# Grouped-query attention over a key-value cache: 512-column scores, block transposes on VectorE, a row maximum, and wo rows loaded apart

## The chip, the cores and the metric

The kernel runs on one core of one Trainium2 chip. The core has a matrix engine (TensorE, PE in the profile, whose weight loads are shown apart as PEld), a vector engine (VectorE, DVE), a scalar engine (ScalarE, ACT), GpSimd (POOL) and SyncE (SP), which here only issues DMA transfers. Sixteen DMA engines move data between the chip's main memory and the on-chip memory SBUF; the matrix engine writes to the accumulator memory PSUM. The metric is the device time of one execution in microseconds (us); smaller is better.

## The reference

```
B, Sq, D = 8, 4, 512;  Hq, Hkv, Sk, Dh = 32, 8, 2048, 128      # all bf16
q = (x @ wq) as [B, Hq, Sq, Dh]
scores = einsum("bhqd,bhkd->bhqk", q, k repeated 4 times) * Dh ** -0.5
p = softmax(scores, axis=-1)
o = einsum("bhqk,bhkd->bhqd", p, v repeated 4 times)
return o as [B, Sq, Hq * Dh] @ wo
```

Each of the 8 key-value heads serves 4 query heads, so a pair (batch, key-value head) has 16 query rows against 2048 keys. The inputs are 33.6 MB of keys, as much of values, 4.2 MB of wq and 4.2 MB of wo; x and the output are 32 KB each.

## The kernel before

The work is cut into 16 units (`units`, L81): unit u is one batch and one group of G = 4 key-value heads. A unit's keys are one transfer of 2 MB (`load_k`, L85), its values another (`load_v`, L93). SBUF partition g * 32 + s holds 64 consecutive keys of head g, 16 KB in all, so each transfer writes 128 partitions with one 16 KB run each.

For the scores the keys must stand with the 128 head dimensions on the partitions. `transpose_part` (L143) does a quarter of a unit (t = 0 to 3): it views two bf16 values as one 4-byte word, transposes 128x128 blocks on TensorE against a 4-byte identity (L151) into a PSUM buffer of the pool `psum_k` (3 buffers), and VectorE copies each half quarter, 1024 bf16 per partition, to the tile `kt` (L152). The two dimensions of a word stay side by side, so q is prepared once as a block form `q_bd` with e = 0 and 1 for the two halves of a word.

`scores` (L212) multiplies, for each head g, each e and each quarter t, a 32-column weight by 256 columns of `kt` (L221, 32 matmuls per unit). Four quarters go to four groups of 32 output partitions. ScalarE takes the exponential of each head's scores and gives the row sums (L229). No maximum is subtracted. `probs_to_keys` (L236) transposes the result on TensorE (L239, 8 per unit) and ScalarE copies four 32-partition pieces into `probs` (L245), which is zero where a key's head is not the query's head. `norms` (L252) sums the row sums over the partitions by a matmul with ones (L261) and takes the reciprocal (L269). `values` (L273) accumulates 64 matmuls with value blocks as weights (L278), and `finish` (L286) scales the result into `oT`.

At the end `to_tokens` (L295) and `to_wo_rows` (L303) bring a half of the heads into the row order in which wo was loaded, and `project` (L312) multiplies by wo. wo has four parts p of 1024 rows; partition q of a part holds 8 consecutive rows of it, r = 0 to 7.

The order of instructions on each engine is the order in the code (`manual_schedule`, L64). The loop at L323 runs stages n = 1 to 17. Stage n transposes unit n's keys, does the scores and probabilities of unit n - 1 and the norms and values of unit n - 2 (w). On TensorE stage n is: quarter 0, scores(n - 1), quarter 1, the norms matmul, quarter 2, values first half, quarter 3, the probability transposes, values second half.

All loads go through SyncE's queue. Keys and values have three buffers each, so a load of unit u is issued when unit u - 3 has been read (the last key transposes, or the last value matmul): `load_ready` at L351 stands at the end of each stage. wo uses the place in SBUF that wq had. Part 0 of wo is loaded as one transfer ahead of the values of unit 14 (L112), and parts 1, 2 and 3 follow the values of unit 15, part 3 in four pieces of 256 KB (L354). The last matmuls wait for the last piece; then ScalarE copies the sum out (L364) and two transfers store it.

## Time and profile before

| what | value |
|---|---|
| median of 3 runs | 190.44 us (190.15 to 190.62) |
| profiled execution: span | 188.4 us; its own time is not listed apart from its span |
| moved by DMA | 75.89 MB, 403 GB/s over the span |
| PE, DVE, ACT busy | 140.1, 103.5, 94.4 us |
| load of keys, of values: issue to landing (median) | 21.8 us, 25.3 us |

The span runs from the program's first instruction to its last; it is 2.0 us under the median of the runs. Busy time of an engine is an average over the whole span, so it does not tell which engine a stage waits for. "Issue to landing" includes the time that a transfer stands behind earlier ones in the queue. Besides the data queue the profile lists queues of kind "instruction": through these the engines get their own programs from main memory, on the same 16 DMA engines.

### The profile page before, as it was taken

How to read it: one execution, taken by the hardware profiler on the slowest of the kernel's cores; microseconds unless marked ns; L12 is line 12 of the kernel's file. 1: busy time of each engine (PE TensorE's matmuls, PEld its weight loads, DVE VectorE, ACT ScalarE, POOL GpSimd, SP SyncE). 2: the span in 40 equal slices, each digit the busy share in tenths (PEclk: the TensorE clock that was granted, in tenths of full speed). 3: DMA queues.
4: the chain of work that ended last, by engine and by line, in shares of the span. 5: the costliest groups of instructions: out<-in, count | busy, mean ns of one | idle time of the engine just before them, and what ended most of it. 6: DMA issues, size and time to landing. Idle time of an engine off the chain costs nothing.

```text
span 188.4 us, 5301 instructions
## 1 busy us (share of the span) xinstructions
PE 140.1 (74%) x2356; PEld 121.5 (65%) x2356; DVE 103.5 (55%) x189; ACT 94.4 (50%) x200; POOL 8.2 (4%) x11
## 2 busy tenths in 40 slices
PE   0290869797979777777777888879777777776681
PEld 0290357696968766767675878777767677665560
DVE  4082286777776656574747457575747565740120
ACT  2000243958476573646556093919292837468500
POOL 8800000000000000000000000000000000000000
PEclk9999678999999999999999699999999999999997
DMA  6998999999999999999999999999999999999940
GB/s 202 466 445 383 428 421 431 428 411 435 431 402 438 426 431 411 431 435 414 421 438 421 431 418 435 418 424 435 421 418 438 419 428 412 414 445 414 399 184 12
DMA packets 5926, 75.89 MB, mean 403 GB/s; under 512 B 688, under 2 KB 784, under 8 KB 1296
## 3 DMA queue, kind: packets, MB, share of 16 engines
q1 hardware_dynamic: 5856, 75.55, 95.2%
q8 instruction: 18, 0.29, 0.6%
q14 instruction: 4, 0.03, 0.0%
q10 hardware_dynamic: 48, 0.02, 0.0%
HBM read 75.53 MB, written 0.03 MB: 401 GB/s over the span
## 4 chain that ended last, share of the span: by engine, by line
DMA 69%; PE 23%; DVE 4%; ACT 1%; issue 1%; SPq 1%
DMA wo_sb<-in_wo_dram 25%; DMA k_sb<-in_k_cache_dram 21%; DMA v_sb<-in_v_cache_dram 14%; PE kp L151 11%; DMA x_sb<-in_x_dram 9%; PE o_ps L278 4%; PE s_ps L221 3%; DVE kt L152 3%; PE psq L176 2%; PE pt L239 1%; PE l_ps L261 1%; ACT q_bd L201 1%; DVE q_bd L201 0%; ACT q_nat L185 0%; DVE by_gq L254 0%
## 5 line engine op out<-in xcount | busy, mean ns | idle before, releaser
L152 DVE COPY kt<-kp 128x1024 bf16<-128x1024 bf16 x128 | 82.0, 682 | 42.7 <-PE kp L151 42.6
L245 ACT COPY probs<-pt 32x1024 bf16<-32x1024 bf16 x64 | 64.2, 1002 | 58.4 <-PE pt L239 57.2
L151 PE MATMUL kp<-ident,k_sb 128*128 128x128 f32 x512 | 71.5, 286 | 16.9 <-DMA k_sb<-in_k_cache_dram 16.6
L151 PEld LDWEIGHTS kp<-ident,k_sb 128*128 128x128 f32 x512 | 59.0, 148 | 22.3 <-issue 13.2
L278 PE MATMUL o_ps<-probs,v_sb 128*128 128x64 bf16 x1024 | 35.7, 195 | 4.4 <-DMA v_sb<-in_v_cache_dram 4.4
L278 PEld LDWEIGHTS <-v_sb 128*128 128x128 bf16 x1024 | 34.0, 99 | 5.2 <-DMA v_sb<-in_v_cache_dram 5.1
L229 ACT ACTIVATE s_sb<-s_ps 128x256 bf16<-128x256 f32 x64 | 23.6, 383 | 2.2 <-PE s_ps L221 1.9
L221 PE MATMUL s_ps<-kt,q_bd 128*32 128x256 bf16 x512 | 18.6, 286 | 0.0
L261 PE MATMUL l_ps<-by_gq,ones 128*128 128x64 f32 x32 | 6.9, 298 | 15.6 <-DVE by_gq L254 15.6
L261 PEld LDWEIGHTS l_ps<-by_gq,ones 128*128 128x128 f32 x32 | 4.8, 188 | 19.3 <-DVE by_gq L254 17.6
L221 PEld LDWEIGHTS <-q_bd 128*32 128x32 bf16 x512 | 12.7, 97 | 3.7 <-issue 2.6
L269 DVE RECIPROCAL r_sb<-l_ps 128x64 f32<-128x64 f32 x16 | 8.9, 557 | 9.0 <-PE l_ps L261 9.0
L229 ACT ACTIVATION_READ_ACCUMULATOR s_sb<-s_ps 128x1 f32 x64 | 13.2, 206 | 0.0
L288 DVE TENSOR_TENSOR oT<-o_ps,r_sb 128x64 bf16<-128x64 f32 x16 | 3.6, 224 | 16.1 <-PE o_ps L278 16.1
L185 ACT ACTIVATE q_nat<-psq 128x512 bf16<-128x512 f32 x2 | 1.2, 597 | 20.0 <-PE psq L176 20.0
L239 PE MATMUL pt<-ident,s_sb 128*128 128x128 bf16 x128 | 9.8, 219 | 0.3 <-ACT s_sb L229 0.3
L239 PEld LDWEIGHTS <-s_sb 128*128 128x128 bf16 x128 | 8.4, 98 | 0.6 <-ACT s_sb L229 0.5
L315 PE MATMUL out_ps<-wo_sb,oP 128*32 128x256 bf16 x64 | 4.5, 274 | 1.0 <-DMA wo_sb<-in_wo_dram 0.5
L364 ACT CAST out_sb<-out_ps 64x256 bf16<-64x256 f32 x1 | 0.4, 365 | 8.2 <-PE out_ps L315 8.2
L315 PEld LDWEIGHTS <-oP 128*32 128x32 bf16 x64 | 3.0, 96 | 2.0 <-issue 0.9
L176 PE MATMUL psq<-wq_sb,xT_sb 128*32 128x512 bf16 x32 | 3.5, 623 | 0.3 <-DVE xT_sb L169 0.3
L134 POOL MEMSET probs<- 128x4096 bf16 x1 | 3.5, 3511 | 0.0
(27 smaller groups left out, 29.1 us busy)
## 6 DMA issues: line engine op xcount, KB each, us to landing
k_sb<-in_k_cache_dram SPq DMA_DIRECT2D x16, 2048.0 KB, 21.8
v_sb<-in_v_cache_dram SPq DMA_DIRECT2D x16, 2048.0 KB, 25.3
wq_sb<-in_wq_dram SPq DMA_DIRECT2D x1, 4096.0 KB, 17.0
wo_sb<-in_wo_dram SPq DMA_DIRECT2D x3, 1024.0 KB, 23.7
wo_sb<-in_wo_dram SPq DMA_DIRECT2D x4, 256.0 KB, 22.3
x_sb<-in_x_dram SPq DMA_DIRECT2D x1, 32.0 KB, 16.7
out_dram<-out_sb SPq DMA_DIRECT2D x1, 16.0 KB, 1.4
out_dram<-out_sb ACTq DMA_DIRECT2D x1, 16.0 KB, 1.6
```

Source lines behind the costliest of these rows:

```text
L151: nc.tensor.transpose(kp[:, j, :], k4[:, w : w + 128], ident4[:, :])
L152: nc.vector.tensor_copy(out=kt[(u, t)][:, half * J // 2 : (half + 1) * J // 2, :, :].rearrange("k j s e -> k (j s e)"), in_=kp[:, :, :].re ...
L176: nc.tensor.matmul(psq[g * T : (g + 1) * T, :], lhsT=xT_sb[:, r, :], rhs=wq_sb[:, r, c0 : c0 + rep * Dh], start=(r == 0), stop=(r == R - 1),)
L221: nc.tensor.matmul(s_ps[t * 32 : (t + 1) * 32, g % 2, :, :], lhsT=q_bd[:, hq, e, g, b, :, :], rhs=kt[(u, t)][:, :, g * S : (g + 1) * S, e] ...
L229: nc.scalar.activation(out=s_sbs[u][:, :, g, :], in_=s_ps[:, g % 2, :, :], func=EXP, accum_out=l_sbs[u][:, g : g + 1],)
L239: nc.tensor.transpose(pt[:, j, :], s_sbs[u][:, j, :, :].rearrange("q g s -> q (g s)"), ident[:, :])
L245: nc.scalar.copy(out=pr[rows, :, g, :], in_=pt[rows, :, :].rearrange("s j (c q) -> s (j c) q", q=HQ),)
L261: nc.tensor.matmul(l_ps[:, :], lhsT=ones[:, :], rhs=by_gq[:, :, :].rearrange("k g q -> k (g q)"), start=True, stop=True,)
L269: nc.vector.reciprocal(r_sbs[u][:, :], l_ps[:, :])
L278: nc.tensor.matmul(o_pss[u][:, :], lhsT=vs[u][:, 2 * (t * J + j) + c, :], rhs=probs[u % 2][:, i, :, :].rearrange("s g q -> s (g q)"), star ...
L288: nc.vector.tensor_tensor(out=oT[hq][:, :, :, b, :].rearrange("d h p s -> d p h s"), in0=o_pss[u][:, :].rearrange("d (p h s) -> d p h s", ...
L315: nc.tensor.matmul(out_ps[half * T : (half + 1) * T, :], lhsT=oP[p // 2][:, r, p % 2, :], rhs=wo_sb[:, p, r, half * DH : (half + 1) * DH], ...
```

## The change

- SBUF is laid out anew: a pad of 384 bytes and the large buffers come first, the small tiles behind. In before the wq/wo, key and value buffers begin 192 bytes past a multiple of 512, in the changed kernel on a multiple of 512.
- The transposed keys are kept as two halves of a unit, 3 buffers of 8 KB in the place of 6 of 4 KB. Of each quarter's two copies VectorE does the first and ScalarE the second. `psum_k` has 4 buffers, the scores' pool one of two banks, and the pool of the probability transposes is gone.
- Scores: 16 matmuls of 512 columns in the place of 32 of 256, with the four heads on the four groups of output partitions. VectorE takes the row maximum over all 1024 scores of a partition, swaps it with the partition that holds the other half of the same row (stream_shuffle), and forms the negated maximum of both. One exponential per unit on ScalarE uses it as bias (new function `exponentials`).
- Probabilities: VectorE transposes 32x32 blocks of 4-byte words and copies four 32-partition pieces; TensorE and ScalarE do nothing there.
- Norms: the same, with one multiplication by a per-partition scalar.
- wo, part 0: the first 640 of its 1024 rows are loaded in two transfers (256 and 384 KB) whose outer dimension in main memory is 8, after the values of units 4 and 10; the other 384 rows keep the old place. `to_tokens` and `to_wo_rows` follow this order of rows for n = 0. The result of `to_wo_rows` is 4-byte in PSUM.
- In a stage the second half of the order is: quarter 1, exponentials, norms, values first half, quarter 2, probs_to_keys, quarter 3, values second half.

```diff
+    align = ctx.enter_context(tc.tile_pool(name="align", bufs=1))
+    align.tile([128, 192], BF16, name="pad")
...
     def load_wo(p, r0, n):
+        rows = wo[p * HP * 128 : (p + 1) * HP * 128, :]
+        if p == 0 and r0 < XR:
+            rows = rows[: 128 * XR, :].rearrange("(b a r) j -> a b r j", a=8, r=XR)
+            nc.sync.dma_start(wo_sb[:, p, r0 : r0 + n, :], rows[:, :, r0 : r0 + n, :])
...
         if u == NU:
-            loads.append(("w", 0))
+            loads.append(("w", (XR, WR - XR)))
         loads.append(("v", u - 2))
+        if u == 6:
+            loads.append(("w", (0, 2)))
+        if u == 12:
+            loads.append(("w", (2, 3)))
...
-            nc.vector.tensor_copy(
-                out=kt[(u, t)][:, half * J // 2 : (half + 1) * J // 2, :, :].rearrange(
+            (nc.scalar.copy if half else nc.vector.tensor_copy)(
+                out=kt[(u, t // 2)][:, j0 : j0 + J // 2, :, :].rearrange("k j s e -> k (j s e)"),
...
+        for tp in range(2):
+            for e in range(2):
+                for g in range(G):
+                    nc.tensor.matmul(
+                        s_ps[g * 32 : (g + 1) * 32, tp, :, :],
+                        lhsT=q_bd[:, hq, e, g, b, :, :],
+                        rhs=kt[(u, tp)][:, :, g * S : (g + 1) * S, e],
...
+        nc.vector.reduce_max(
+            out=top[:, :],
+            in_=s_ps[:, :, :, :].rearrange("q t j s -> q (t j s)"),
+            axis=AX,
+        )
+        nc.vector.stream_shuffle(swapped[:, :], top[:, :], [i ^ HQ for i in range(32)])
+        nc.vector.tensor_scalar(
+            out=less[u][:, :], in0=swapped[:, :], scalar1=top[:, 0:1], scalar2=-1.0,
+            op0=mybir.AluOpType.max, op1=MULT,
+        )
...
+    def exponentials(u):
+        nc.scalar.activation(
+            out=s_sbs[u][:, :, :, :].rearrange("q a s j -> q a j s"),
+            in_=s_pss[u][:, :, :, :].rearrange("q t (a j) s -> q (t a) j s", j=2),
+            func=EXP, bias=less[u][:, 0:1], accum_out=l_sbs[u][:, :],
+        )
...
     def probs_to_keys(u):
-        for j in range(J):
-            nc.tensor.transpose(
+        nc.vector.transpose(
...
         for g in range(G):
-            nc.scalar.copy(
+            nc.vector.tensor_copy(
...
         if n < NU:
             transpose_part(n, 1)
+        if n - 1 < NU:
+            exponentials(n - 1)
         if w >= 0:
             norms(w)
-        if n < NU:
-            transpose_part(n, 2)
...
         if n < NU:
-            transpose_part(n, 3)
+            transpose_part(n, 2)
         if n - 1 < NU:
             probs_to_keys(n - 1)
+        if n < NU:
+            transpose_part(n, 3)
```

## The prediction

> **What bounds the kernel now.** I read the shares of the engines and the slices, then the DMA queues, the chain that ended last, and the timeline of one stage and of the end.
>
> ```profile
> PE 140.1 (74%) x2356; PEld 121.5 (65%) x2356; DVE 103.5 (55%) x189; ACT 94.4 (50%) x200; POOL 8.2 (4%) x11
> ...
> DMA  6998999999999999999999999999999999999940
> ...
> q1 hardware_dynamic: 5856, 75.55, 95.2%
> q8 instruction: 18, 0.29, 0.6%
> q14 instruction: 4, 0.03, 0.0%
> ...
> DMA 69%; PE 23%; DVE 4%; ACT 1%; issue 1%; SPq 1%
> ```
>
> DMA is busy from the second slice to the last but two, and holds 69% of the chain. A stage moves two loads of 2 MB; at the 428 GB/s of the middle slices that is 9.8 us. The page's DMA row is a mean of 16 engines, so I took from the trace when each engine's share of the last wo load arrived (us from the span's start):
>
> ```
> 179.68 179.70 179.73 179.81 180.04 180.09 | 181.12 181.78 | 182.73 182.76 182.80 182.91 182.92 182.96 | 184.57 184.58
> ```
>
> Sixteen engines with equal shares end up to 4.9 us apart. In the records every q8 packet (16 KB) makes one engine about 1.55 us later than the rest, and the packets go round eight engines in turn. 18 packets are two rounds and two more: six engines 3.1 us late (two packets), two 4.8 us late (three), the other eight not at all, save for two that q14 packets delay by 1.2 and 1.9. q8 carries PE's program: (2356 + 2356) / 18 = 262 PE instructions per packet. The first group's 4.72 MB per engine at 613 ns per 16 KB packet take 176.7 us, which from its first packet at 1.8 us leaves about 1 us to 179.7: it streamed with hardly a hole, so SP's queue never ran dry; the bound is the last engine.
>
> ```profile
> 119.24 1.06 PE L151 MATMUL kp<-ident,k_sb 128*128 128x128 f32 x8 [0.47 <-DMA k_sb<-in_k_cache_dram]
> ...
> 123.93 0.56 DVE L269 RECIPROCAL r_sb<-l_ps 128x64 f32<-128x64 f32 x1 [0.53 <-PE l_ps L261]
> ...
> 177.04 2.04 PE L278 MATMUL o_ps<-probs,v_sb 128*128 128x64 bf16 x64 [1.60 <-DMA v_sb<-in_v_cache_dram]
> ...
> 183.97 0.40 PE L315 MATMUL out_ps<-wo_sb,oP 128*32 128x256 bf16 x4 [0.26 <-DMA wo_sb<-in_wo_dram]
> ...
> 184.62 0.39 PE L315 MATMUL out_ps<-wo_sb,oP 128*32 128x256 bf16 x4 [0.26 <-DMA wo_sb<-in_wo_dram]
> ```
>
> The stage waits for its keys by 0.5 us, the end for the last two wo pieces by 0.26 each: DMA leads, compute follows closely. The sum goes against the span, 188.4; the median is 2.04 longer, which I keep.
>
> **Fewer PE instructions.** Per unit 16 of 32 score matmuls and all 8 probability transposes go, each with its weight load. Over the built program that is 2340 - 1964 = 376 matmuls and as many loads: 4712 - 752 = 3960, by 262 gives 15 packets. That is under two rounds, so the third delay of the two slowest engines goes: last arrival 182.96 in the place of 184.58, -1.6 us.
>
> **640 wo rows with outer dimension 8.** No load of before has such a dimension, so its spread is not shown. If 16 engines still share it, nothing moves. If eight do, each of these gets 16 pieces of 2 KB (84 ns in the packet records) and 16 of 3 KB (about 122): 3.3 us, in the place of 5/8 of eight 8 KB pieces of 312 ns, 1.56. So +1.74 us on eight and -1.56 on the others. If the eight are those without q8 packets, the arrivals become 180.09 + 1.74 = 181.8, 182.9 and 183.5 for the two with q14 packets, and 182.96 - 1.56 = 181.4 for the rest. ACT's program shrinks from 176 to 128 instructions, so one q14 delay (0.6 to 0.9) may go: 182.9 to 183.5, against 184.58 a gain of 1.1 to 1.7. If they are the eight with q8 packets: 182.96 + 1.74 = 184.7, no gain at all. The Trainium skill, "DMA: Bandwidth & Descriptors", section "Why a DMA increments its semaphore by 16 and not by 1", has a load from SP cut over the largest number up to 16 that divides both outer dimensions, on the lowest-numbered engines: eight here. No run so far shows it, nor which eight fetch PE's program.
>
> **The pad.** The buffers move from 192 past 512 to a multiple of it. Packets of 16 KB take 613 ns, and wq's of 32 KB 1213, 606.5 per 16 KB: from nothing to 1% of 175 us, 1.9 us. Both addresses were equally off in before, so I take little, -0.2, and keep 1.9 for the range.
>
> **VectorE's new chain.** VectorE loses 64 of 128 `kt` copies and gains the maximum, the transposes and the `probs` copies. Rows:
>
> ```profile
> L152 DVE COPY kt<-kp 128x1024 bf16<-128x1024 bf16 x128 | 82.0, 682 | 42.7 <-PE kp L151 42.6
> ...
> L254 DVE TENSOR_TENSOR by_gq<-l_sb,by_q 128x64 f32<-128x64 f32 x16 | 3.4, 215 | 0.0
> ...
> L186 DVE TENSOR_SCALAR q_nat<-psq 128x512 bf16<-128x512 f32 x2 | 1.4, 692 | 3.6 <-ACT q_nat L185 3.6
> ...
> L310 DVE COPY oP<-perm 128x512 bf16<-128x512 bf16 x2 | 0.8, 423 | 1.3 <-PE perm L307 1.3
> ```
>
> L186 over 512 4-byte elements from PSUM is 692, so 1024 are 1.23 us. From one maximum to the next: maximum 1.23; shuffle and negation 0.45 (two small ones under L254's 215); `kt` copy 0.645 (pairs take 1.29); weighting 0.2; then the wait 0.53, the reciprocal 0.56 and the wait for values and quarter 2 (1.10 + 0.5 - 0.56), 2.15 in all; copy 0.645; block transpose 0.64 (between a copy's 0.34 and twice that rate's 1.2; taken at one element per cycle as L186); four `probs` copies; copy 0.645; `finish` 0.22; copy 0.645, during which the last half of the scores runs. Without the four: 7.5 us. A `probs` copy has 512 4-byte elements per partition: between L310 (0.42) and L186 (0.69); I take 0.42, a copy like it: 9.2 us, with 0.69 it is 10.2. Both lie beside the load's 9.8, the first under it. ScalarE has four copies of 1.0 (L245) and one exponential of about 1.2: 5.2 us per stage, hidden.
>
> What waits behind: the maximum stalls every later DVE copy, so PE's norms stand 2 us idle per stage, and the key buffer is free at PE's quarter 3, some 8 us after its start against 7.4. The next key load but two is issued that much later; at 32.8 us it was issued with the queue full until about 42, so SP's and DMA's order keeps 8 us in hand. The two added issues on SP (0.33 us each) stand before such waits and cost nothing. The tail's fp32 `perm` copy takes 0.69 for 0.42: +0.27 in the chain from the last values (177.04) to the last piece, which waits twice 0.26, so hidden; if that cover goes, 0.27 is added.
>
> **The sum.** 188.4 - 1.3 - 0.2 = 186.9, plus 2.04: 188.9 us.
>
> **Rivals.** (a) The eight engines are those that fetch PE's program: the two gains cancel, 190.5, no change; for it, nothing in before ties the fetching engines to a number. (b) The load still uses 16 engines: -1.6 - 0.2, 188.6. (c) VectorE's chain becomes the stage. Stage 2's scores stand at 34.0 in before; DVE's new work in stage 1 puts the first maximum at about 37. Unit 14's scores are at 160.5 in before, 13 stages later, so a stage may take 123.5 / 13 = 9.5 us; above that every tenth costs 1.3 us at the end. At 9.7 it is +2.6 less the 1.3: 191.7; at 10.2 it is +9: 198. For it: 9.2 is near, and PE's clock:
>
> ```profile
> 98.00:108.00 10.00, 7.98 (x102) 7.06 (x103) 5.13 (x9) 3.82 (x11) 0.00 (x0) 0.83 1.02 431
> 118.00:128.00 10.00, 8.45 (x155) 7.53 (x151) 6.64 (x12) 5.79 (x13) 0.00 (x0) 1.00 1.02 431
> ```
>
> A stretch whose PE gaps were only 1.05, 1.08 and 0.83 us was granted 0.83 of the clock; the changed stage has one gap of 2 us and a lower PE share. Each slow stage would add about 1 us. The Trainium skill, "TensorE: Matmul & The Clock Gate", section "Part 1: The HAM clock gate", has the clock fall after an idle window of 3.4 us; by that no stage would slow and (c) would lose this support, but the trace shows the fall at shorter gaps. Against (c): VectorE is busy 7.6 of 9.8 us, and 8 us of queued loads absorb single slow stages.
>
> **How the numbers follow.** Forecast 0.46; (a) 0.16; (b) 0.08; (c) 0.30, centred on 192 with a tail to 199. Low end: the forecast with the pad's full 1.9, 187.2. High end: (c) at 9.8 us per stage, 193.0; beyond that 0.1 is left. Leading case alone: 187.2 to 189.6. A measurement tells 0.3%, 0.57 us. Faster: forecast and (b), 0.54; same: (a), 0.16; slower: 0.30.
>
> **What would show it.** q8 with 15 packets; the last arrivals within 3 us of each other; `probs` copies near 0.42 us; a wait of PE for `k_sb` in most stages (right) or of PE and DVE for each other with none for `k_sb` (c). Wrong if the DMA row thins, or a stage exceeds 9.8 us.

## The result, and the profile after

The changed kernel takes 195.94 us (median of 4 executions, 193.5 to 202.82) against 190.53 (190.15 to 190.71) for the kernel before: 2.8% slower by the medians, and slower by a ratio of 1.0163 with a 95% interval of 1.0139 to 1.0188. The ratios here and below compare executions within 1.5% of the fastest one of their kernel, so this one leaves out 198.2 and 202.82 (that of e17, which has only one such execution, takes all four). The forecast was 188.9 with a range of 187.2 to 193.0. The profiled execution is the one of 193.5 us, with a span of 191.7 against 188.4.

The page of the changed kernel: slices, a queue, the chain.

```profile
PEclk9999799999999999999999999999975999997899
DMA  6999999999999999999999999999999999999920
GB/s 191 465 438 397 431 434 427 427 424 422 438 427 434 427 405 357 438 429 434 424 424 427 427 434 427 432 431 344 330 420 434 431 431 431 420 427 418 378 80 9
...
q8 instruction: 15, 0.25, 0.5%
...
DMA 44%; PE 26%; DVE 23%; ACT 2%; issue 2%; SPq 0%; DVEq 0%
```

The 15 packets of q8 are there, as forecast (q14 kept its 4). The DMA row still reads 9 from end to end, but the row below it does not: 357 in the slice at 72 us, 344 and 330 at 130 to 139. A DMA engine that is busy need not move much. VectorE had 4% of the chain and now has 23%.

Stretches around the two loads that use an outer dimension of 8 (their packets run at 70.9 to 73.8 and 131.5 to 136.9 us), and one behind them. The last three columns are TensorE's clock, the DMA share and GB/s.

```profile
66.00:70.00 4.00, 3.67 (x63) 3.13 (x65) 3.86 (x9) 2.36 (x3) 0.00 (x0) 1.00 1.03 442
70.00:75.50 5.50, 3.15 (x57) 2.40 (x46) 3.39 (x8) 2.93 (x4) 0.00 (x0) 1.00 1.01 346
...
131.00:138.50 7.50, 5.88 (x105) 5.02 (x98) 5.84 (x13) 4.89 (x6) 0.00 (x0) 1.00 1.02 315
...
142.00:148.00 6.00, 5.42 (x32) 3.58 (x32) 2.21 (x6) 1.01 (x1) 0.00 (x0) 0.50 1.01 431
```

All sixteen DMA engines are busy in the stretches of the two loads and move 346 and 315 GB/s in the place of about 430. Against 430 that is 0.46 and 0.86 MB, or 1.1 and 2.0 us of all sixteen. In the packet records the pieces of 2 and 3 KB take 120 and 184 ns on average, but the 16 KB packets slow down too, from 611 ns to 725 and 820 on average of those that start there.

TensorE's timeline from the second of these loads to the end (start, duration, work, and in brackets the wait before it and what ended it).

```profile
142.58 1.94 PE L171 MATMUL kp<-ident,k_sb 128*128 128x128 f32 x8 [3.87 <-DMA k_sb<-in_k_cache_dram]
144.45 1.90 PE L238 MATMUL s_ps<-kt,q_bd 128*32 128x512 bf16 x16
...
157.81 0.44 PE L300 MATMUL l_ps<-w_gq,ones 128*128 128x64 f32 x2 [1.55 <-DVE w_gq L294]
...
166.74 0.43 PE L300 MATMUL l_ps<-w_gq,ones 128*128 128x64 f32 x2 [1.54 <-DVE w_gq L294]
...
172.47 0.62 PE L238 MATMUL s_ps<-kt,q_bd 128*32 128x512 bf16 x8 [1.06 <-DVE kt L172]
175.02 0.49 PE L300 MATMUL l_ps<-w_gq,ones 128*128 128x64 f32 x2 [1.94 <-DVE w_gq L294]
175.30 3.57 PE L317 MATMUL o_ps<-probs,v_sb 128*128 128x64 bf16 x64
...
180.70 2.09 PE L317 MATMUL o_ps<-probs,v_sb 128*128 128x64 bf16 x64
...
186.11 1.92 PE L380 MATMUL out_ps<-wo_sb,oP 128*32 128x256 bf16 x32 [0.78 <-DVE oP L375]
```

The keys behind the second load come late and TensorE waits 3.87 us; then its clock is at half (0.50 from 142 to 148 us, the last of the stretches), and the transposes take 1.94 for 1.06. From there no stage waits for a load again: the norms matmuls, which wait for VectorE, stand 8.93 us apart. In the last stage TensorE waits 1.06 and 1.94 us with 0.62 of work between, the clock falls again (0.57 from 175 to 179), and the values of unit 14 take 3.57 us in the place of the 2.09 of unit 15. The end waits for VectorE's `oP`, not for wo.

How far the loads and how far the compute set the end can be read from two numbers: when the last packet of wo ends, and how much of the span lies behind it. In before they are 184.15 and 4.2. Here they are 185.56 and 6.2. So of the 3.4 us of span, 1.4 came with the loads and 2.0 with the compute behind them.

### The profile page after: what moved, and what is told of

Same layout as the page of the kernel before. It is cut to its first block, busy times and chain, and to the rows that moved or that the text cites. A ratio compares the mean times of both kernels' runs of the same rounds, so it can differ in the third digit from the quotient of the medians.

```text
span 191.7 us, 4519 instructions
## 1 busy us (share of the span) xinstructions
PE 133.4 (70%) x1980; PEld 107.8 (56%) x1980; DVE 128.1 (67%) x271; ACT 89.9 (47%) x104; POOL 8.2 (4%) x11
## 4 chain that ended last, share of the span: by engine, by line
DMA 44%; PE 26%; DVE 23%; ACT 2%; issue 2%; SPq 0%; DVEq 0%
DMA k_sb<-in_k_cache_dram 36%; DMA x_sb<-in_x_dram 9%; PE kp L171 9%; DVE kt L172 7%; PE o_ps L317 7%; DVE top L248 6%; DVE probs L285 4%; PE s_ps L238 3%; PE l_ps L300 2%; PE out_ps L380 2%; DVE p_t L277 2%; PE psq L194 2%; DVE less L254 1%; DVE w_gq L294 1%; DVE swapped L253 1%
## 5 line engine op out<-in xcount | busy, mean ns | idle before, releaser
L172 ACT COPY kt<-kp 128x1024 bf16<-128x1024 bf16 x64 | 63.1, 1014 | 73.3 <-PE kp L171 73.3
L172 DVE COPY kt<-kp 128x1024 bf16<-128x1024 bf16 x64 | 43.8, 687 | 25.9 <-PE kp L171 25.4
L285 DVE COPY probs<-p_t 32x512 f32<-32x512 f32 x64 | 26.8, 419 | 1.3
L267 ACT ACTIVATE s_sb<-s_ps,less 128x1024 bf16<-128x1024 f32 x16 | 22.5, 1407 | 4.6 <-DVE less L254 4.6
L300 PE MATMUL l_ps<-w_gq,ones 128*128 128x64 f32 x32 | 6.9, 298 | 24.3 <-DVE w_gq L294 24.3
L248 DVE TENSOR_REDUCE top<-s_ps 128x1 f32<-128x1024 f32 x16 | 19.5, 1220 | 6.1 <-PE s_ps L238 6.0
L238 PE MATMUL s_ps<-kt,q_bd 128*32 128x512 bf16 x256 | 19.0, 398 | 2.9 <-DVE kt L172 2.9
L300 PEld LDWEIGHTS l_ps<-w_gq,ones 128*128 128x128 f32 x32 | 4.8, 188 | 28.2 <-DVE w_gq L294 21.7
L277 DVE STREAM_TRANSPOSE p_t<-s_sb 128x512 f32<-128x512 f32 x16 | 11.2, 702 | 0.8 <-ACT s_sb L267 0.8
L238 PEld LDWEIGHTS <-q_bd 128*32 128x32 bf16 x256 | 4.8, 96 | 11.5 <-DVE kt L172 6.5
```

The costliest lines, as they stand in the source:

```text
L172: (nc.scalar.copy if half else nc.vector.tensor_copy)(out=kt[(u, t // 2)][:, j0 : j0 + J // 2, :, :].rearrange("k j s e -> k (j s e)"), in ...
L238: nc.tensor.matmul(s_ps[g * 32 : (g + 1) * 32, tp, :, :], lhsT=q_bd[:, hq, e, g, b, :, :], rhs=kt[(u, tp)][:, :, g * S : (g + 1) * S, e], ...
L248: nc.vector.reduce_max(out=top[:, :], in_=s_ps[:, :, :, :].rearrange("q t j s -> q (t j s)"), axis=AX,)
L267: nc.scalar.activation(out=s_sbs[u][:, :, :, :].rearrange("q a s j -> q a j s"), in_=s_pss[u][:, :, :, :].rearrange("q t (a j) s -> q (t a ...
L277: nc.vector.transpose(p_t[:, :, :, :].rearrange("s x q j -> s (x q j)").bitcast(FP32), s_sbs[u][:, :, :, :].rearrange("q a s j -> q (a s j ...
L285: nc.vector.tensor_copy(out=pr[rows, :].rearrange("s (x g q) -> s x g q", g=G, q=HQ)[:, :, g, :], in_=p_w[rows, :].rearrange("s (x q) -> s ...
```

## The experiments

Theories at the start: C, the two loads with an outer dimension of 8, over eight engines, hold up all sixteen; D, VectorE's chain sets the end; S, the small pieces or their place in the queue do it. One table holds all runs; ratios are against before on the same chip, which lay between 189.89 and 191.0. "Past" is the span behind the last wo packet of the profiled execution. Kernels with one time ran once.

| run | what differs | us, median (range) | ratio (95%) | last packet | past |
|---|---|---|---|---|---|
| before | | 190.53 (190.15-190.71) | 1 | 184.15 | 4.2 |
| changed kernel | | 195.94 (193.5-202.82) | 1.0163 (1.0139-1.0188) | 185.56 | 6.2 |
| e1 | changed, 640 rows plain, 16 engines | 192.64 (189.98-195.29) | 1.0089 (1.0054-1.0124) | 181.19 | 7.0 |
| e2 | changed, wo loaded as in before | 190.16 (188.13-192.52) | 0.9975 (0.9937-1.0013) | 181.21 | 5.2 |
| e3 | before, with the new wo loads | 198.27 (196.82-199.49) | 1.0419 (1.0349-1.049) | 188.15 | 6.9 |
| e4 | before, with the new layout | 189.22 (188.57-193.66) | 0.9939 (0.9915-0.9962) | 186.94 | 4.9 |
| e5 | changed, four loads of 32 partitions each | 197.87 | | 187.56 | 8.5 |
| e6 | e2, pad 64 bytes | 191.59 (189.5-192.05) | 1.0053 (1.0022-1.0084) | 182.82 | 7.4 |
| e7 | e6, no maximum | 188.8 (188.73-189.0) | 0.9932 (0.9917-0.9947) | 182.92 | 4.2 |
| e8 | e6, last copies on ScalarE | 190.48 (189.1-191.55) | 1.0016 (0.9991-1.004) | 182.65 | 6.0 |
| e9 | changed, eight engines, near rows | 201.34 | | 192.96 | 6.6 |
| e10 | changed, outer dimension 16 | 196.11 | | 185.03 | 9.3 |
| e11 | e6, idle TensorE work in the last stage | 190.23 (189.31-191.13) | 0.9995 (0.9949-1.0041) | 182.78 | 6.5 |
| e12 | e2, idle work and norms moved | 196.38 (196.09-196.72) | 1.0319 (1.03-1.0338) | 184.70 | 10.2 |
| e13 | e6 with four extra loads | 200.93 | | 195.06 | 4.1 |
| e14 | e13, extra loads in reverse order | 202.8 | | 194.86 | 6.2 |
| e15 | changed, pad 64 bytes | 198.48 (197.58-199.67) | 1.0426 (1.0382-1.047) | 186.52 | 9.3 |
| e16 | e2, no maximum | 187.5 (187.0-188.4) | 0.9858 (0.9821-0.9895) | 181.35 | 4.1 |
| e17 | changed, no maximum | 196.25 (192.31-198.69) | 1.031 (1.0263-1.0358) | 185.98 | 4.6 |
| e18 | e1, no maximum | 191.26 (189.68-193.29) | 1.0026 (0.9997-1.0055) | 184.93 | 5.1 |

### Undoing one part, doing one part (e1 to e4)

```diff
 e1, in load_wo, p == 0 and r0 < XR:
-  rows = rows[: 128 * XR, :].rearrange("(b a r) j -> a b r j", a=8, r=XR)
+  rows = rows[: 128 * XR, :].rearrange("(q r) j -> q r j", r=XR)
 e2: load_wo and the list of loads as in before, to_tokens and to_wo_rows in before's row order
-  loads.append(("w", (XR, WR - XR)))      # and (0, 2), (2, 3) early
+  loads.append(("w", (0, WR)))
 e3: before, with the changed kernel's load_wo, list of loads, to_tokens and to_wo_rows
 e4: before, with the changed kernel's order of the pools and
+  align.tile([128, 192], BF16, name="pad")
```

> The changed kernel with one edit: the first 640 wo rows are loaded at the same two places and in the same 2 and 3 KB pieces, but partition q takes rows 5q to 5q+4, so the outer dimension in main memory is 128 and all 16 DMA engines take part. Theory C (the two loads on eight engines hold up all 16: in the changed kernel's trace the rate falls from 431 to about 250 GB/s for 3.5 and 6 us around them, 1.36 MB less than at full rate, 3.15 us): the holes vanish, the last wo arrival comes some 3 us earlier, and the time falls from 193.5 to 188 to 190. Theory D (VectorE's chain of 8.95 us per stage sets the end): the time stays at 192 to 194. Theory S (the small pieces, or their place among the key and value loads, cause the holes): the holes and 193.5 stay.

> The changed kernel with wo loaded as in before: part 0 in one 1 MB transfer ahead of the values of unit 14, with before's row order in the two functions at the end. All the rest is as changed. Theory C: as in the run with 16 engines, 188 to 190. Theory D: 192 to 194. Theory S: 188 to 190, and lower than the run with 16 engines by what small pieces cost. This run also gives the rest of the change by itself: 15 PE program packets for 18 (by the prediction 1.6 us) and the aligned buffers (0 to 1.9 us) against VectorE's chain.

> Before, with nothing but the wo part of the change: 640 rows in two loads with outer dimension 8, the other 384 rows at the old place, and the row order at the end that follows from it. Compute is before's, with 8.7 us per stage. Theory C: the same two holes, so the last wo arrival is up to 3.1 us later, less what the shift of bytes between engines gives back: 192 to 194. Theory D: no loss, 189 to 191. Theory S: as C.

> Before, with nothing but the new layout of SBUF: a pad of 384 bytes and the large buffers first, so that key, value and wo buffers begin on a multiple of 512 bytes instead of 192 past one. If the alignment is why the changed kernel's 16 KB packets take 611 ns where before's take 613 to 620 (607 against 613 from start to start), the last arrival comes 0.8 to 1.0 percent of 175 us earlier, 1.4 to 1.8 us: 188.7 to 189.1. If the packet times have another cause: 190.5.

e3 settles that the new loads alone make a kernel slower: 4.2%, with the same two holes and the last packet 4.0 us later, in a kernel that has nothing else of the change but what goes with them.

```profile
70.00:76.50 6.50, 5.40 (x94) 4.65 (x83) 4.41 (x9) 2.46 (x9) 0.00 (x0) 1.00 1.00 335
132.00:141.50 9.50, 6.20 (x81) 5.46 (x70) 4.66 (x9) 1.94 (x9) 0.00 (x0) 0.87 1.01 309
```

It is later than either theory had it (196.82 to 199.49, with 192 to 194 expected): 2.7 us more than in before lie behind the last packet too, though it has no maximum. Its last keys reach TensorE at 165.5 us, in before at 158.4, and the compute behind them sets the end. e1 has the same pieces of 2 and 3 KB at the same places in the queue: they take 84 and 121 ns, the 16 KB packets of these stretches 615 and 614, nothing is lost, and the last packet ends 4.4 us earlier than in the changed kernel. S is out; C stands for the loads.

e1 and e2 end their last packet at the same time (181.19, 181.21), yet e1 is later: 189.98 against 188.2 in the profiled executions, 192.64 against 190.16 in the median, where theory C had 188 to 190 for both. The last scores of e2 and of e1 in TensorE's timeline:

```profile
167.50 0.62 PE L225 MATMUL s_ps<-kt,q_bd 128*32 128x512 bf16 x8 [1.06 <-DVE kt L159]
```

```profile
168.97 0.62 PE L238 MATMUL s_ps<-kt,q_bd 128*32 128x512 bf16 x8 [1.06 <-DVE kt L172]
```

640 rows moved ahead of the last keys make these 1.47 us later (655 KB at 430 GB/s are 1.52). Where the end follows the last keys through compute, bytes moved ahead of them cost their full time, though the loads as a whole end no later.

e2 answers D: with the loads as in before the last packet ends 2.9 us earlier than in before, but the time does not follow (0.9975): 5.2 us lie behind the last packet, not 4.2, and that in one of its fastest executions; the later ones have no profile. So there are two losses, one in the loads, one in the compute at the end. The layout (e4) gains 0.6% in four of six executions, but e2 and e4 spread over 4 and 5 us where before spreads over 1.

### What makes a load harmful (e5, e9, e10, e13, e14)

e5 cuts each of the two loads into four of 32 partitions.

```diff
 e5
-  rows = rows[: 128 * XR, :].rearrange("(b a r) j -> a b r j", a=8, r=XR)
-  nc.sync.dma_start(wo_sb[:, p, r0 : r0 + n, :], rows[:, :, r0 : r0 + n, :])
+  for c in range(4):
+      part = rows[c * 32 * XR : (c + 1) * 32 * XR, :].rearrange("(b a r) j -> a b r j", a=8, r=XR)
+      nc.sync.dma_start(wo_sb[c * 32 : (c + 1) * 32, p, r0 : r0 + n, :], part[:, :, r0 : r0 + n, :])
 e9 (from e1): pieces of an engine 5 rows apart; some rows of wo then stand in the wrong place
+  rows = rows[: 8 * 17 * XR, :].rearrange("(a b r) j -> a b r j", a=8, r=XR)
+  nc.sync.dma_start(wo_sb[:, p, r0 : r0 + n, :], rows[:, :16, r0 : r0 + n, :])
 e10: a=16 in the place of a=8
```

> The changed kernel with each of the two eight-engine loads of wo cut into four loads of 32 partitions, the same rows in the same 2 and 3 KB pieces to the same places, still over eight engines; only the partitions that one engine writes at a time change (4 neighbours in each load instead of 16). Theory E (eight engines that write 16 neighbouring partitions get in the way of all the others at SBUF): the two holes in the DMA row (242 to 285 GB/s for 3.5 us at 71 us, about 260 for 6 us at 131.5) shrink to the 1.7 us of the larger share, rates stay over 380, and the last loads arrive 2 to 3 us earlier. Rival M (small pieces read by eight engines are slow as such, wherever they land): the holes stay as they are, within 20% of the 1.36 MB that they lacked.

> The changed kernel with the two loads of 640 wo rows still over eight engines and in the same 2 and 3 KB pieces, but with the 16 pieces of one engine 5 rows (5 KB) apart in main memory instead of 40 rows (40 KB): it reads 640 of the first 680 rows, so some rows of wo stand in the wrong place and part of the product is wrong. Theory F (pieces 40 KB apart are what makes main memory slow for everyone): the two holes vanish, no stretch of 1 us under 400 GB/s at 71 to 75 and 131 to 138 us, and the last wo load arrives about 3 us earlier than in the changed kernel. Rival G (eight engines alone make it, as they write 16 neighbouring partitions or only load half the engines): the holes stay, 1.1 to 1.6 MB short in all.

> The changed kernel with the outer dimension of the 640 wo rows 16 in the place of 8: the same rows and 2 and 3 KB pieces, sixteen engines with 8 pieces each, and the pieces of one engine 80 KB apart. Theory F (far pieces): the holes stay, 250 to 300 GB/s for some us at both loads. Rival G (eight engines): no holes, all stretches over 400 GB/s, as in the run with plain rows over sixteen engines.

The stretches of the loads in e5 (the second load is cut where its rate changes), the second load of e9, and both of e10:

```profile
72.50:78.50 6.00, 3.80 (x58) 3.00 (x51) 2.91 (x7) 3.08 (x4) 0.00 (x0) 0.94 1.01 366
...
133.50:135.50 2.00, 2.00 (x32) 1.58 (x34) 1.39 (x3) 0.32 (x1) 0.00 (x0) 1.00 1.00 406
135.50:140.50 5.00, 3.40 (x60) 2.77 (x53) 2.91 (x7) 3.05 (x4) 0.00 (x0) 1.00 1.02 290
```

```profile
138.50:146.00 7.50, 5.88 (x82) 4.84 (x82) 5.93 (x13) 3.96 (x5) 0.00 (x0) 1.00 1.01 306
```

```profile
69.50:75.50 6.00, 4.30 (x66) 2.97 (x63) 5.29 (x14) 3.92 (x4) 0.00 (x0) 1.00 1.02 355
130.00:138.50 8.50, 4.54 (x62) 3.37 (x61) 4.42 (x11) 3.37 (x4) 0.00 (x0) 0.90 1.01 301
```

None of the theories named in these three expectations held. Near rows over eight engines (e9) have the holes, and so have far rows over sixteen engines (e10). So neither the distance of the rows nor the number of engines makes them. e5 loses little less (0.37 and 0.73 MB against 428 GB/s, the changed kernel 0.45 and 0.85), but not evenly: in its second load 0.04 MB in the first 2 us, when the parts for the lower partitions are first in the queue, and 0.69 later. That suggested the partitions. e13 and e14 put four extra loads of 384 KB, all in 128 pieces of 3 KB, into the kernel of e6 and change only where eight engines write.

```diff
 e13: after the values of units 4, 7, 10, 13, into wo's place, which is loaded over later
+  "plain": nc.sync.dma_start(wo_sb[:, 3, 0:3, :], rows.rearrange("(q r) j -> q r j", r=XR)[:, 0:3, :])
+  "lower" (q0 = c % 2 * 32) and "upper" (q0 = 64 + c % 2 * 32), for c in range(4):
+      part = rows[c * 32 * XR : (c + 1) * 32 * XR, :].rearrange("(b a r) j -> a b r j", a=8, r=XR)
+      nc.sync.dma_start(wo_sb[q0 : q0 + 32, 3, r0 : r0 + 3, :], part[:, :, 0:3, :])   # r0 = c // 2 * 3
+  "eight": rows.rearrange("(b a r) j -> a b r j", a=8, r=XR) to 128 partitions
 e14: the same four in reverse order
```

> The run with the pad of 64 bytes (old wo loads) with four extra loads of 384 KB each, in 128 pieces of 3 KB, into wo's place, three stages apart; what they bring is written over later. In this order: plain rows over sixteen engines; eight engines into partitions 0 to 63 alone (four loads of 32 partitions); the same eight engines, rows and pieces into partitions 64 to 127 alone; eight engines as in the changed kernel, 128 partitions. Theory P (a load is harmful where its engines write partitions that belong to other engines in the plain loads; the lowest eight engines own partitions 0 to 63): no loss at the first and the second, under 0.15 MB each against the steady rate, and a loss of 0.8 MB or more at the third, as much as or more than at the fourth. Rival Q (eight engines, or far pieces, are harmful wherever they write): the second loses as much as the third. The Trainium skill, "DMA: Bandwidth & Descriptors", section "The descriptor swizzle", gives engines 0 to 7 the partitions 0 to 63 and engines 8 to 15 the others in a load of 128 partitions.

> The same four extra loads in the reverse order: eight engines and 128 partitions, partitions 64 to 127 alone, partitions 0 to 63 alone, plain rows. Theory P: losses at the first two, none at the last two, so that the place in the run plays no part. Rival Q: losses at the first three.

The four stretches of e13 in order (plain, lower, upper, eight), then those of e14 (eight, upper, lower, plain):

```profile
70.00:75.00 5.00, 3.49 (x61) 2.60 (x58) 3.88 (x10) 3.38 (x4) 0.00 (x0) 1.00 1.02 423
101.00:106.00 5.00, 3.49 (x58) 2.99 (x51) 3.14 (x8) 2.78 (x4) 0.00 (x0) 1.00 1.00 419
132.00:141.50 9.50, 7.79 (x124) 6.58 (x122) 7.18 (x16) 5.35 (x7) 0.00 (x0) 1.00 1.02 288
166.00:176.00 10.00, 6.75 (x78) 5.51 (x77) 5.36 (x13) 3.68 (x5) 0.00 (x0) 0.83 1.02 313
```

```profile
70.00:78.00 8.00, 5.84 (x93) 4.38 (x90) 5.79 (x15) 4.13 (x5) 0.00 (x0) 1.00 1.02 283
104.00:112.50 8.50, 5.74 (x68) 4.90 (x61) 4.91 (x11) 3.80 (x5) 0.00 (x0) 0.85 1.02 274
138.50:145.00 6.50, 4.90 (x76) 3.83 (x75) 4.95 (x11) 3.53 (x5) 0.00 (x0) 1.00 1.00 421
164.00:175.00 11.00, 8.41 (x150) 7.25 (x151) 8.00 (x17) 6.01 (x8) 0.00 (x0) 1.00 1.01 424
```

| 384 KB written | lost against 428 GB/s, e13 and e14 | one 3 KB piece | 16 KB packets that start in the stretch |
|---|---|---|---|
| plain, 16 engines | 0.03, 0.04 MB | 124, 123 ns | 621, 617 ns |
| 8 engines, partitions 0-63 | 0.05, 0.05 MB | 123, 124 ns | 616, 616 ns |
| 8 engines, partitions 64-127 | 1.33, 1.31 MB | 227, 228 ns | 879, 924 ns |
| 8 engines, 128 partitions | 1.15, 1.16 MB | 206, 249 ns | 785, 865 ns |

Theory P (a load is harmful where its engines write partitions that belong to other engines in the plain loads) holds, wherever the load stands. The loss is (428 less the GB/s) times the length of the stretch shown. The same pieces of the same rows cost next to nothing in the lower half of the partitions and 3.1 us of all sixteen engines in the upper half (1.33 MB at 428 GB/s). The Trainium skill, "DMA: Bandwidth & Descriptors", section "The descriptor swizzle", gives each engine eight partitions of its own in a load of 128, the lowest eight engines those of the lower half; that fits each row of the table, and e10, where sixteen engines, if each takes eight neighbouring partitions, are off that map. e10 also speaks against a simpler rule, that the lowest eight engines must keep to the lower half: if its engines take the partitions in order, they do, and the holes are there. The map itself was not read from a trace here: the packet records do not name the engine.

### The end (e6, e7, e8, e11, e12, e16)

```diff
 e6, from e2
-    align.tile([128, 192], BF16, name="pad")
+    align.tile([128, 32], BF16, name="pad")
 e7, from e6 (e16 the same from e2): no reduce_max, stream_shuffle, tensor_scalar, and
-            bias=less[u][:, 0:1],
 e8, from e6, in transpose_part
-            (nc.scalar.copy if half else nc.vector.tensor_copy)(
+            (nc.scalar.copy if half or t == 3 else nc.vector.tensor_copy)(
 e11, from e6, behind each half of the last scores
+            if u == NU - 1:
+                warm(14 if tp else 8)      # so many transposes of ident4 into a free psum_k buffer
 e12, from e2: warm(8) twice, and in the loop
+        if n == NU:
+            norms(w)                       # ahead of scores(n - 1)
```

> The changed kernel with all of wo loaded as in before (as in the run with the old wo order) and the pad at 64 bytes in the place of 384, so that the large buffers begin 192 bytes past a multiple of 512 again. Theory A (the place of the buffers makes the spread between runs): all runs lie within 0.5% of each other, 16 KB packets take 613 to 620 ns, and the time is 188 to 189.5, as VectorE's chain still sets the end. Rival (the spread comes from the compute of the new stage, with its lower clock): the runs still spread over 188 to 192.5.

> As the run with the pad of 64 bytes, without the row maximum, its swap and its negation, and with no bias in the exponential: the softmax's maximum is left out. VectorE's chain gets some 1.7 us shorter per stage (1.22 for the maximum, two small ones of about 0.25). Theory D (at the end of the kernel VectorE's chain is behind the loads and sets the time): the end follows the last loads again, 1.5 to 2.5 us earlier than in the run with the maximum, and TensorE's last waits are for wo. Rival (the loads set the end): no change over 0.5 us.

> As the run with the pad of 64 bytes, with both copies of the last quarter of the transposed keys on ScalarE, nothing left out. VectorE's chain gets 0.69 us shorter per stage (one copy of 687 ns), ScalarE gets 1.01 longer. Theory D: the last units run at up to 0.69 us less each, and the end comes 0.5 to 1.5 us earlier than in the run with the pad of 64 bytes. Rival (the chain runs over TensorE's last quarter, not over VectorE's copy): no change, or up to 0.5 us later because the copy of 1.01 us on ScalarE is longer than the 0.69 on VectorE.

> As the run with the pad of 64 bytes (old wo loads; 191.59, between 189.5 and 192.05), with idle work for TensorE in the last stage alone: 8 transposes of the identity between the halves of the last scores and 14 behind them, where it waits 1.06 and 1.94 us for VectorE; nothing waits for these. Theory H (the spread and the late end come from TensorE's clock, which falls in these two waits behind the row maximum): no slice at half clock in the last 20 us, the matmuls of the last values take 2.1 us in the place of 3.2 to 3.6, the end follows the last loads again, 188.5 to 189.3, and the runs lie within 0.5%. Rival (VectorE's chain itself makes the end late): 190 or more, spread as before.

> The changed kernel with the old wo loads and its own pad (190.16, between 188.13 and 192.52), with idle transposes for TensorE in the last stage (8 between the halves of the last scores, 8 behind them) and, in that stage alone, the norms of unit 14 ahead of the scores of unit 15, so that they no longer stand behind the row maximum on VectorE. Theory H: the end follows the last loads, whose last packet ends at about 181.2; span about 185.4, 187.0 to 187.5 in most runs, and one run in some is 3 us longer where the loads fall to 376 GB/s for a while. Rival: no change against 190.16.

> The run without the row maximum (188.8, old wo loads, pad of 64 bytes) with the changed kernel's pad of 384 bytes; the softmax's maximum is left out as in before, which has none. The end of that run followed the loads, and with this pad the last packet ended 1.6 us earlier where nothing was in the way: 187.0 to 187.5 in most runs. If this pad's loads fall to 376 GB/s at times, some runs lie 2 to 6 us higher and the spread is over 1%, where the run with the pad of 64 bytes had 0.15%.

The end of e6 on TensorE:

```profile
168.88 0.62 PE L225 MATMUL s_ps<-kt,q_bd 128*32 128x512 bf16 x8 [1.06 <-DVE kt L159]
171.44 0.69 PE L287 MATMUL l_ps<-w_gq,ones 128*128 128x64 f32 x2 [1.94 <-DVE w_gq L281]
171.92 3.62 PE L304 MATMUL o_ps<-probs,v_sb 128*128 128x64 bf16 x64
176.02 0.69 PE L287 MATMUL l_ps<-w_gq,ones 128*128 128x64 f32 x2 [0.48 <-DVE w_gq L281]
176.63 1.89 PE L346 MATMUL out_ps<-wo_sb,oP 128*32 128x256 bf16 x16
178.46 3.19 PE L304 MATMUL o_ps<-probs,v_sb 128*128 128x64 bf16 x64
```

The last packet is in at 182.82, 1.3 us before that of before, but the end is 7.4 us behind it. The wait of 1.94 us before the norms stands behind the row maximum on VectorE (the 1.06 is for a copy of the last keys, and e7 has it too). After these waits the clock is at half: 3.62 and 3.19 us for two lots of values that take 2.09, 1.89 for a projection of 1.05. Without the maximum (e7) the span behind the last packet is 4.2 again, the time 188.8, and four executions lie within 0.15%. Its end:

```profile
170.62 3.58 PE L286 MATMUL o_ps<-probs,v_sb 128*128 128x64 bf16 x64 [0.92 <-DMA v_sb<-in_v_cache_dram]
...
183.39 0.40 PE L328 MATMUL out_ps<-wo_sb,oP 128*32 128x256 bf16 x4 [0.23 <-DMA wo_sb<-in_wo_dram]
```

The first line shows that the clock falls without the maximum too (e4, with before's compute, has 3.57 us behind one wait of 1.43); but the last matmuls of e7 wait for wo, so this fall is hidden. That the place of the buffers made e2 spread was wrong: e6 has before's place and spreads too. e16, e7 with the layout of the changed kernel, ends at 187.0 to 188.4; its last wait is for wo:

```profile
179.64 1.85 PE L328 MATMUL out_ps<-wo_sb,oP 128*32 128x256 bf16 x28 [0.78 <-DVE oP L323]
181.72 0.39 PE L328 MATMUL out_ps<-wo_sb,oP 128*32 128x256 bf16 x4 [0.23 <-DMA wo_sb<-in_wo_dram]
```

e8 takes one copy of 687 ns off VectorE's stage and gains 1.1 us in the median on e6, within what theory D had, though the intervals of the two ratios overlap. e11 tells the clock from the chain: with TensorE kept busy in the two waits the first lot of values takes 2.08, but the fall comes one wait later.

```profile
171.73 2.08 PE L311 MATMUL o_ps<-probs,v_sb 128*128 128x64 bf16 x64
175.76 0.51 PE L294 MATMUL l_ps<-w_gq,ones 128*128 128x64 f32 x2 [1.95 <-DVE w_gq L288]
176.19 1.89 PE L353 MATMUL out_ps<-wo_sb,oP 128*32 128x256 bf16 x16
178.01 2.68 PE L311 MATMUL o_ps<-probs,v_sb 128*128 128x64 bf16 x64
```

Its four executions are two at 189.3 to 189.4 and two at 191.1, so the spread stays and the 188.5 to 189.3 of theory H is missed. The theory was half right: the clock is part of the late end, the chain (maximum, exponential, block transposes, four copies, weighting) the other.

Between 15 us and the last matmul the clock of all the profiles is at half for 3.4, 6.8 or 10.2 us at a time. In the last 20 us it is 10.2 us in e5, e6, e10 and e15, with 7.4 to 9.3 us behind the last packet; one fall of 3.4 in the changed kernel, e1, e2, e7, e8, e9 and e11, with 4.2 to 7.0; none in e16, e17 and e18, with 4.1 to 5.1. (e12 does not fit: two falls of 3.4 from 172 us on, and 10.2 us behind the last packet.) So the length of the fall may be what makes some executions of one kernel late; as only one execution of each has a profile, this is not shown. e12 failed (196.38, with 187.0 to 187.5 expected), and taught the same: the norms moved ahead of the last scores wait 1.99 us for `w_gq`, which stands on VectorE behind the copies of quarter 3, so the last scores themselves came later. Its profiled execution also shows something that came with the new layout:

```profile
22.00:46.00 24.00, 17.43 (x218) 12.66 (x210) 19.66 (x41) 15.11 (x19) 0.00 (x0) 1.00 1.01 378
46.00:70.00 24.00, 18.00 (x291) 15.53 (x292) 17.50 (x38) 13.15 (x17) 0.00 (x0) 1.00 1.00 427
```

From 16 to 48 us all sixteen engines are busy at 378 GB/s, and then at 427, with nothing in the program to tell the two apart. Of the eleven profiles with the buffers on a multiple of 512, five (e4, e5, e9, e12, e18) have such a stretch in the first 80 us; of the nine with the buffers 192 past it, before among them, none has. The kernels differ in other things too, so this is a link, not a cause that one edit has shown. Why all four executions of e12 are late is open: its profile has the stretch, but also 10.2 us behind the last packet.

### Where both meet (e15, e17, e18)

```diff
 e15: the changed kernel with align.tile([128, 32], ...)
 e17: the changed kernel without the maximum (as e7)
 e18: e1 without the maximum
```

> The changed kernel with its pad cut from 384 to 64 bytes, so that the large buffers begin 192 bytes past a multiple of 512 as in before; the eight-engine loads stay. If the place of the buffers makes the changed kernel's later times (198.2 and 202.8 beside 193.5 and 193.7): no run over 196, 16 KB packets at 613 to 620 ns outside the two holes, and a median of 194 to 195, some 1.5 us over the changed kernel's best for the slower packets. If not: runs of 198 and more appear here too.

> The changed kernel, eight-engine loads included, without the row maximum (left out, as in before). If the loads lose 3.1 us for all engines and the eight carry 1.7 us more bytes, whatever VectorE does: the last packet ends near 185.6 as in the changed kernel, the span is about 189.5 to 190.5 and the time 191.3 to 192.3, some 4 us over the same kernel with the old loads (187.5); the spread between runs shrinks to about 1%. If the loss needed VectorE's chain, it is under 189.

> The same without the maximum, with the 640 rows loaded early as plain rows over sixteen engines. If loading early costs nothing of itself: 187.0 to 188.4, as with the old loads. If the last keys, which then come 1.5 us later (640 KB at 430 GB/s), set the end also without the maximum: 189 and more.

e15 says that the changed kernel's execution at 198.2 needs no slow stretch: with before's place of the buffers all four are at 197.6 to 199.7, the profiled one with 9.3 us behind the last packet and TensorE at half clock from 176 to 186 us. The one at 202.82 lies above all of these, and its cause is open. e17's profiled execution, 192.31, is where it was expected: last packet at 185.98, 4.6 us behind it, 5.1 us of span over e16. Its other three (195.6 to 198.7) are later than expected and have no profile, so their cause is open too; they do not need the maximum. e18 has 189.68 to 193.29, the "189 and more" of the case where the later keys set the end also without the maximum, but it does not settle this: its profile fell on a stretch of about 385 GB/s from 20 to 54 us. One long wait does not always make the clock fall: in the last stage of e17, between two lots of values, TensorE waits longer than anywhere in the last stage of e6, and the values behind it take their 2.09.

```profile
177.79 0.43 PE L282 MATMUL l_ps<-w_gq,ones 128*128 128x64 f32 x2 [2.13 <-DVE w_gq L276]
...
179.14 2.09 PE L299 MATMUL o_ps<-probs,v_sb 128*128 128x64 bf16 x64
```

## Why the prediction was wrong

**The step that failed is "640 wo rows with outer dimension 8".** It weighed bytes per engine, +1.74 us on eight and -1.56 on the others, with the packets at the 84 and about 122 ns of plain loads, and so stood in the sum with about +0.3 us (-1.3 with the shorter program, which alone had -1.6). That it is eight engines fits the trace: the semaphore of each such load has one update about 1.1 us after the issue and then eight single ones (for the first load from 73.33 to 74.16 us), which is what the Trainium skill, "DMA: Bandwidth & Descriptors", section "Why a DMA increments its semaphore by 16 and not by 1", has for a load on eight. The packets took 120 and 184 ns, and what the step put at nothing is the effect on the other engines' packets: 3.1 us of all sixteen in the changed kernel, which comes, as e13 and e14 show, from where in SBUF the eight write. With the uneven shares the last packet is 4.4 us later than in e1, in the place of +0.3. As a whole the new loads cost 4.2% on before (e3) and 1.9% on e2. The forecast span of 186.9 has its last packet at 182.65 (184.15 less the 1.5 of the sum); of the 4.8 us that the profiled execution is longer, 2.9 lie in the loads and 1.9 behind them.

**The second failure is "what waits behind".** The chain of VectorE was sized well: a stage that waits for nothing else takes 8.93 us (9.2 forecast), the `probs` copy 419 ns (420), the maximum 1220 (1230), the block transposes 702 (640).

```profile
L285 DVE COPY probs<-p_t 32x512 f32<-32x512 f32 x64 | 26.8, 419 | 1.3
...
L248 DVE TENSOR_REDUCE top<-s_ps 128x1 f32<-128x1024 f32 x16 | 19.5, 1220 | 6.1 <-PE s_ps L238 6.0
```

It was hidden in each stage, as put. But after the last keys there is no next load to hide it. The forecast priced only the `perm` copy in the tail; the maximum and the 1.94 us wait behind it stand there too, and the clock falls as well. With the old loads the maximum is worth 2.8 us between the medians of e6 and e7, and takes back what the loads gain. In the changed kernel it is 1.6 us of the span behind the last packet (6.2 against 4.6 in e17), and nothing in the median (195.94 against 196.25).

**Fewer PE instructions** fits: 15 packets, last packet 1.2 to 1.5 us earlier in e6, e7, e8 and e11 (1.6 forecast), though no run changes the number of packets alone; and where the end follows the loads the time follows: e7 is at 188.8 against before's 190.2. **The pad** was taken too low: 1.6 us earlier from e6 to e2, inside its bounds of 0 and 1.9, at the price of the slow stretches. **The key buffer** cost nothing that the profiles show. **The `perm` copy** does cost what the forecast gave it for a lost cover: the wait for `oP` before the last matmuls is 0.78 us where before has 0.52, and in the changed kernel, e2 and e6 no wait for wo hides it.

**The rivals.** The times of (a) and (b), 190.5 and 188.6, did not come about; whether the eight engines of these loads are those that fetch PE's program was not read from a trace. (c) was put as VectorE's chain above 9.5 us per stage; no stage got there, so its mechanism did not act as put, though its time, 191.7 at 9.7, was nearer than the forecast's. The support it drew from the clock was real but acted elsewhere: one wait of 3.87 us for keys and the waits of the last stage. That the Trainium skill's rule in "TensorE: Matmul & The Clock Gate", section "Part 1: The HAM clock gate", names an idle window of 3.4 us fits the 3.87; in the last stage the longest single wait was 1.94, and the clock fell all the same, so here the trace decides: shorter waits close together can do it too.

**The signs the prediction named.** The 15 packets and the `probs` copies came as put. The last arrivals were to lie within 3 us of each other; the last wo load's sixteen came from 180.13 to 186.42 us, further apart than in before. TensorE waited 7 times for `k_sb` in 16 units, not in most stages. "Wrong if the DMA row thins" was the wrong row: the DMA share stayed full, only GB/s fell.

## What to carry to other kernels

A load whose engines write other partitions than in a plain load of 128 can slow every transfer beside it: price it by what it does to its neighbours, and read GB/s and the packets' durations, not the busy share. Work that is hidden in every stage has to be priced a second time in the last one, where no load is left to hide it and short waits in a row can cost half of TensorE's clock for some us. Of this change the parts that helped, as far as the runs show, were the shorter program and the layout: with the old wo loads and without the maximum, which before does not have either, the kernel is at 187.5 us, 0.9858 of before (0.9821 to 0.9895); with before's place of the buffers at 188.8, and that within 0.15%.

## What was not expected of the hardware

- Eight engines that write 384 KB to partitions 64 to 127 cost all sixteen the time of 1.33 MB (288 GB/s over 9.5 us in e13); to partitions 0 to 63 the same pieces cost 0.05 MB.
- With the buffers on a multiple of 512 bytes the median 16 KB packet takes 611 ns in the place of 613 (e4 against before), but five of eleven profiles run the loads at about 380 GB/s for some 28 to 62 us from about 16 us on, with packets of 676 to 701 ns, and then recover at once. What begins and ends such a stretch is open.
- TensorE's clock was halved after waits of 1.06 and 1.94 us with 0.62 us of work between them, for 3.4 us in the changed kernel, e1 and e2 and for 10.2 in e6; after 1.06 and 2.13 us with 2.9 us between them (e17) it was not.
